# Attention weights and u turned by TensorE instead of by transposing transfers, with ScalarE, VectorE and GpSimd sharing the rest differently

## The chip, the cores and the metric

The kernel runs on one core of one Trainium2 chip. The metric is device time in microseconds. TensorE (PE in the profile) multiplies and turns matrices and writes to PSUM. VectorE (DVE), ScalarE (ACT) and GpSimd (POOL) do the elementwise work. SyncE (SP) issues transfers. Each engine takes its instructions in the order in which the program gives them.

## The reference, cut to what matters

```python
# q, k, v: (8 batches, 8 heads, 576 rows, 64), fp32; tau = 0.02
scores = scale * np.matmul(q, k.transpose(0, 1, 3, 2))          # 576 x 576 for each head
thresh = np.max(scores, axis=-1, keepdims=True) - tau
scores = np.where(scores >= thresh, scores, -1000000000.0)
scores = scores - np.max(scores, axis=-1, keepdims=True)
attn = np.exp(scores)
attn = attn / (np.sum(attn, axis=-1, keepdims=True) + 1e-09)
x = np.matmul(attn, v)                                          # heads side by side: (8, 576, 512)

xt = x.transpose(0, 2, 1)
h = xt @ U @ V                                                  # U: 576 x 32, V: 32 x 576
u = x + h.transpose(0, 2, 1)
ch = np.maximum(u @ w_ch1, 0.0) @ w_ch2                         # 512 x 2048 and 2048 x 512
out = u + ch
```

## The kernel before

There are eight batches of four pairs of heads, 32 pairs in all. The rows of a head are five tiles (four of 128 and one of 64; the short tiles of two pairs are put together), so that two pairs are nine steps, and the whole is 144 steps of two tiles each, 288 tiles of attention weights.

**Loads and preparation.** Each pair's q and k are loaded (L510), turned by TensorE in fp32 (L572, L585) and copied to `qkT` by ScalarE (L578, L591). `LOADERS` says for the first pairs which queue issues the loads; GpSimd issues the others. The values are split in bf16: ScalarE makes the high part `vh` (L600), GpSimd the low part (L607).

**A step.** TensorE multiplies scores for two heads, two steps at a time after the first pairs (L641), into the two tiles `trio` of PSUM, which hold six of its eight banks. For each of the two tiles VectorE scales and copies the scores to SBUF and takes their extreme (L670). ScalarE makes the threshold of both tiles, the extreme plus tau (L686), and the exponentials (L693). VectorE selects what passes the threshold and sums it up (L700), with the weights in bf16 going into `w_ring`. GpSimd copies 64 columns of a tile to fill a whole block (`twin`, L718). Then the tile, 128 x 640, must be turned for the product with the values. This is done in one of two ways:

- by a transposing transfer on SP's queue (`turn_w`, L724), of two tiles at a time, or one where the other goes the second way;
- by TensorE, five passes of 128 x 128 into a bank of PSUM (`turn_pe`, L731), and a copy to SBUF by ScalarE (`copy_w`, L741). So it is for 25 tiles: the second tile of steps 1 to 3 of the first eight pairs (`EARLY`), and one other.

`w_ring` holds four steps.

**A pair.** The turned tiles `wT_ring` and `wT4` are multiplied with `vh` (L800, L804, L808), the results put together by ScalarE and VectorE (L855, L859) and divided by the sums on GpSimd (L866). The first four pairs (`SOFT`) have one product with the inverse sums instead, on VectorE (L831). The inverse of the sums is two instructions of VectorE (L774 adds 1e-9, L776 inverts). Then follow the low-rank part (L871 to L885, L894), the sum u on VectorE (L901), its rounding to bf16 on ScalarE (L908), and the turning of u into `uT`: for the first eight pairs by TensorE (L916) with a copy by ScalarE (L932), for the other 24 by a transposing transfer on SP's queue (L922).

**A batch.** `mixer_tasks` multiplies `uT` with the first weight (`up`, L998, and `rest`, L1014), ScalarE takes the positive part (L988), TensorE multiplies with the second weight (`down`, L1031), and VectorE adds u from PSUM to SBUF (`finish`, L1043), from where it is sent out (L1054 to L1060).

**The order.** Every operation is a task, and the list `ORDER` gives the sequence in which the tasks are issued, `BANK` the PSUM bank of each that needs one. Negative numbers in `ORDER` are fillers, matmuls of an identity whose result is not used (L473). Costs and due times in the tasks served to make the lists; when the kernel is built, only the lists count:

```python
        for n in ORDER:
            if n < 0:
                self.filler(-1 - n)
                continue
            t = self.tasks[n]
```

Of the kernel before, what the change touches and what calls it, by code (L numbers as in the profile page):

```python
# [68 lines left out]
P = 128  # L69
FP32 = mybir.dt.float32  # L70
# [15 lines left out]
EARLY = 8  # L86
PHASES = (1, 2, 3, 4, 5, 6, 8, 28)
LONE = 2
LOADERS = (None, "SSSS", "SSSS")
ACTED = 0  # L90


W1_AT = (1, 4, 6, 9, 11, 14, 16, 19)
W2_AT = (20, 21, 23, 24, 25, 26, 28, 29)
# [14 lines left out]
PE, VEC, SCA, POOL, SP = range(5)  # L109
# [3 lines left out]
class Task:  # L113
# [17 lines left out]
    23, 21, 22, 25, 20, 26, 24, 19, 44, 28, 46, 40, 27, 29, 42, -1, -1, -1, -1, -1, -1, -1, -1, -1, 32, 41, 30, 33,  # L131
    43, 34, 31, 39, 35, 45, -2, -2, -2, 59, 201, 36, 200, 60, 37, 38, 204, 61, 63, -7, -7, -7, -7, -7, 69, 205, 62,
    65, 64, 206, 54, 70, 50, 198, 55, 52, 71, 203, 73, 218, 82, 66, 72, 202, 77, 222, 74, 199, 1, 83, 47, 67, 3, 84,
    49, 86, -3, -3, -3, -3, -3, -3, 95, 0, 78, 68, 85, 51, 87, 53, 90, 96, 75, 97, 219, 76, -8, -8, -8, -8, -8, -8,
    108, 91, 221, 98, 99, 2, 48, 211, 103, 109, 207, 209, 110, 112, 119, 100, 225, 212, 111, 104, 79, 114, 213, 120,
    92, 224, -3, 80, 121, 123, 220, -7, 129, 115, 125, 223, 113, 122, 4, 93, 131, 432, 56, 130, 101, 210, 88, 439,
    142, 89, 124, 137, 105, 81, 126, 57, 106, 102, 94, 143, 169, 132, 127, 144, 437, 146, 128, 155, 168, 214, 150,
    138, 107, 233, 170, 139, 231, 116, 157, 145, 438, 133, 117, 229, 156, 232, 457, 238, 134, 163, 455, 208, 151,
    158, 234, 171, 434, 230, 240, 159, 135, 58, 136, 239, 140, 244, 147, 152, 241, -6, 248, 141, 118, 172, 456, 242,
    245, 5, 243, 433, 153, 249, 453, 154, 250, 160, -8, -8, -8, -8, 173, 251, 164, 215, 161, 174, 256, 452, 261, -1,  # L140
    -1, -1, 184, 162, 148, 252, 262, 435, 264, 183, 149, 165, -4, 273, 257, 459, 175, 185, 246, 258, 253, 247, 216,
    274, 176, 254, 458, 275, 228, 177, 263, 268, 217, 286, -8, -8, 178, 255, 166, 259, 281, 179, 443, 454, 277, 269,
    188, 226, 436, 276, 287, 444, 227, 6, 180, 189, 265, 167, -3, -3, -3, -3, -3, -3, 181, 278, 288, 266, 289, 296,
    282, 270, 260, 267, 182, 290, 283, 291, 297, 441, 279, 271, 186, 292, 280, 300, 298, 272, 293, 345, 235, 440,
    344, 187, 299, 306, 294, 236, 302, 447, 445, 237, 307, 284, 448, 309, 346, 308, 301, 626, 446, 462, -2, -2, -2,
    318, 285, 303, 295, 190, 310, 304, 460, 313, 319, 191, 320, 9, 192, 322, -8, -8, 193, 331, 311, 347, 326, 624,
    312, 194, 321, 620, 334, 314, 349, 305, 195, 467, 348, 315, 625, 350, 468, 332, -4, 316, 351, 465, 333, 339,
    352, 335, 463, 353, 466, 196, 323, 336, 354, 317, 472, 355, 324, 464, 619, 325, 327, 356, 337, 622, 197, 474,
    357, 328, 338, 442, 623, 473, 364, 358, 461, 621, 329, 340, 475, 476, 482, 639, 359, 478, 341, 477, 640, 330,
    365, 8, 483, 342, 484, 360, 10, 343, 495, 7, 486, 362, 496, 449, 642, 479, 485, 507, 469, 363, 487, 490, 470,  # L150
    361, 498, 509, 480, 634, 366, 488, 481, 630, 471, 508, 632, 635, 631, 521, 367, 644, 633, 489, 520, 368, 497,
    511, -7, -7, 369, 491, 530, 522, 510, 370, 515, 492, 645, 499, 371, 887, 502, 531, 882, 372, 374, 532, 373, 12,
    493, 375, 494, 641, 380, 503, 533, 523, 376, 540, 504, 381, 11, 505, 525, 516, 378, 500, 377, 512, 886, 501,
    382, 506, 526, 450, 379, 384, 383, 541, 534, 13, 386, 524, 536, 513, 552, 535, 527, 514, 385, 537, 542, 883,
    387, 543, 528, 517, 538, 553, 646, 518, 547, 650, 554, 451, 519, 388, 529, 566, 555, 14, 390, 628, 565, 389,
    888, 651, 659, 544, 391, 556, 545, 884, 392, 546, 660, 560, 661, 394, 567, 568, 629, 548, 393, 669, 647, 561,
    395, 549, 539, 572, 557, 643, 665, 670, 562, 550, 558, 663, 648, 16, 396, 671, 551, 627, 885, 573, 398, 397,
    569, 672, 400, 662, 399, 682, 570, 673, 574, 402, 571, 881, 683, 401, 563, 674, 403, 652, 559, 654, 564, 578,
    577, 901, 598, 653, 666, 15, 655, 649, 575, 677, 694, 664, 579, 678, 685, 667, 580, 689, 679, 695, 581, 892,
    576, 696, 902, 684, 894, 698, 18, 707, 896, 582, 893, 690, 675, 897, 702, 586, 708, 676, 583, 599, 895, 584,  # L160
    587, 636, 585, 588, 717, 668, 686, 903, 600, 601, 589, 710, 691, 637, 712, 718, 17, 607, 590, 719, 603, 687,
    638, 697, 727, 608, 709, 680, 703, 656, 591, 904, 889, 692, 404, 699, 604, 907, 592, 890, 681, 609, 704, 406,
    602, 605, 688, 693, 728, 606, 405, 593, 765, 713, 906, 407, 723, 711, 908, 739, 766, 610, 594, 700, 611, 657,
    767, 701, 714, 595, 905, 740, 612, 658, 715, 912, 752, 613, 720, 596, 729, 614, 721, 741, 1048, 705, 911, 408,
    734, 1054, 722, 716, 597, 1049, 409, 724, 706, 1051, 753, 410, 742, 747, 725, 615, 1055, 726, 411, 730, 735,
    913, 914, 412, 743, 736, 769, 1053, 731, 915, 413, 616, 773, 744, 732, 770, 916, 737, 774, 748, 917, 617, 1072,
    755, 733, 921, 775, 754, 749, 764, 738, 771, 794, 776, 909, 618, 923, 768, 750, 795, 414, 922, 745, 759, 772,
    746, 796, 1068, 924, 415, 760, 751, 1071, 925, 891, 756, 931, 1050, 927, 926, 1052, 777, 785, 757, 932, 1075,
    786, 758, 933, 1070, 941, 778, 761, 934, 787, 416, 779, 942, 935, 780, 788, 898, 417, 781, 944, 928, 762, 950,
    763, 936, 929, 937, 418, 797, 782, 930, 899, 951, 946, 790, 789, 952, 900, 910, 960, 1063, 1059, 791, 954, 1061,  # L170
    792, 1057, 961, 783, 793, 943, 420, 1062, 1056, 938, 1069, 953, 784, 421, 1280, 947, 1064, 1060, 939, 970, 956,
    945, 1278, 940, 798, 955, 948, 957, 918, 949, 799, 962, 971, 919, 422, 800, 965, 1277, 972, 806, 1058, 974, 801,
    1073, 966, 423, 963, 1074, 807, 426, 958, 802, 920, 808, 959, 427, 981, 803, 1279, 973, 424, 428, 985, 1273,
    980, 804, 809, 964, 429, 805, 976, 975, 967, 811, 982, 810, 430, 1009, 968, 983, 986, 977, 989, 1010, 1078, 812,
    1011, 978, 1008, 1274, 979, 990, 1083, 1079, 991, 993, 969, 1013, 984, 1080, 425, 995, 813, 999, 987, 1014,
    1000, 843, 992, 988, 1084, 814, 1015, 1001, 1017, 996, 1002, 1088, 994, 1065, 1018, 1004, 1066, 1081, 1019,
    1003, 1016, 815, 1082, 1089, 844, 1037, 1020, 1090, 819, 997, 1038, 998, 1039, 1091, 1005, 816, 817, 1094, 1006,
    1098, 1076, 1012, 1092, 1095, 1293, 1007, 818, 1093, 1295, 820, 1021, 1099, 1275, 821, 431, 1276, 1100, 1022,
    822, 1298, 1029, 1028, 1077, 1108, 1023, 1104, 1067, 1024, 1109, 823, 1030, 1101, 1031, 1102, 1096, 1281, 1296,
    1105, 1117, 824, 1097, 1294, 1103, 1110, 1113, 1299, 1025, 1111, 1106, 1282, 1297, 1118, 1288, 1284, 1107, 1300,  # L180
    1119, 1289, 1286, 1285, 1127, 1033, 1441, 1287, 1128, 1123, 1040, 845, 1112, 1034, 1120, 1085, 1137, 1035, 1124,
    846, 1121, 1114, 1026, 1139, 1115, 825, 1129, 1447, 1130, 1116, 1138, 1036, 827, 1143, 1122, 1032, 826, 829,
    1148, 1140, 1141, 1125, 831, 1442, 1147, 1126, 830, 1086, 1131, 828, 847, 832, 1149, 1156, 1132, 1142, 1041,
    1133, 848, 1157, 1134, 1150, 1308, 1087, 1135, 1042, 1158, 1309, 1304, 1043, 1152, 1166, 1306, 1176, 1305, 1027,
    1167, 1467, 1307, 1175, 1440, 1168, 1044, 1151, 1159, 833, 1283, 1177, 1443, 1178, 1302, 1313, 1446, 1144, 834,
    1303, 1160, 1045, 1145, 1180, 1466, 1146, 1315, 1465, 1314, 835, 1181, 1445, 1169, 1153, 1323, 1461, 1162, 1161,
    1179, 1316, 1182, 836, 1163, 1171, 1184, 1324, 1319, 1164, 1444, 1204, 1325, 1185, 1317, 837, 1154, 1464, 1170,
# [186 lines left out]
def kernel(  # L374
# [24 lines left out]
    nc.vector.tensor_copy(out=identb, in_=ident)  # L399
    tau_t = consts.tile([P, 1], FP32, name="tau_t")  # L400
    nc.vector.memset(tau_t, tau_f)

    warm = consts.tile([P, 1], FP32, name="warm")
    nc.scalar.activation(out=warm, in_=tau_t, func=ACT.Exp)

# [761 lines left out]
```

## Time and profile before

| | |
|---|---|
| runs of the kernel | 602.58 and 609.11 us, median 605.85 us |
| profiled execution | 601.79 us, span 600.0 us |
| PE busy | 574.2 us, 96% of the span |
| DVE busy | 515.7 us, 86% |
| ACT busy | 459.4 us, 77% |
| POOL busy | 337.1 us, 56% |
| granted TensorE clock | full in all 40 slices |
| transfers issued on SP's queue that turn tiles or u | 167: 127 to `wT_ring`, 16 to `wT4`, 24 to `uT` |
| packets of the queue that carries them | 212544, 69.2% of the time of the 16 DMA engines |

The span runs from the first instruction to the last, and the device time contains a little more. Busy shares are of the span. Matmuls overlap on PE, so that a busy PE can have room, and the time of a stretch of matmuls is better read from the distance of their starts than from the length of one.

### The profile page before, as it was taken

How to read it: one execution, taken by the hardware profiler on the slowest of the kernel's cores; microseconds unless marked ns; L12 is line 12 of the kernel's file. 1: busy time of each engine (PE TensorE's matmuls, PEld its weight loads, DVE VectorE, ACT ScalarE, POOL GpSimd, SP SyncE). 2: the span in 40 equal slices, each digit the busy share in tenths (PEclk: the TensorE clock that was granted, in tenths of full speed). 3: DMA queues.
4: the chain of work that ended last, by engine and by line, in shares of the span. 5: the costliest groups of instructions: out<-in, count | busy, mean ns of one | idle time of the engine just before them, and what ended most of it. 6: DMA issues, size and time to landing. Idle time of an engine off the chain costs nothing. (4 is left out here: it accounts for less than half of the span.)

```text
span 600.0 us, 16926 instructions
## 1 busy us (share of the span) xinstructions
PE 574.2 (96%) x6150; PEld 346.3 (58%) x6221; DVE 515.7 (86%) x1399; ACT 459.4 (77%) x959; POOL 337.1 (56%) x580
## 2 busy tenths in 40 slices
PE   7999999899999998999999999999999999999996
PEld 4466655665665664656565665556655666555542
DVE  3999999999999999999999999999988999962002
ACT  3788999898898876997679986799786887683330
POOL 2987777787467558664567474576473544141000
PEclk9999999999999999999999999999999999999999
DMA  5999999986999899998898998998999877684203
GB/s 118 177 159 153 177 156 183 167 173 136 155 164 168 156 173 177 175 160 155 162 176 159 170 154 184 192 167 167 157 174 142 176 135 138 97 155 74 62 19 88
DMA packets 226996, 90.49 MB, mean 151 GB/s; under 512 B 205408, under 2 KB 217520, under 8 KB 226912
## 3 DMA queue, kind: packets, MB, share of 16 engines
q1 hardware_dynamic: 212544, 67.48, 69.2%
q0 software_dynamic: 13408, 21.58, 17.7%
q8 instruction: 49, 0.80, 0.6%
q10 hardware_dynamic: 960, 0.34, 0.2%
q14 instruction: 35, 0.29, 0.2%
HBM read 37.90 MB, written 9.44 MB: 79 GB/s over the span
## 5 line engine op out<-in xcount | busy, mean ns | idle before, releaser
L693 ACT ACTIVATE e_sb<-s_sb,m 128x576 bf16<-128x576 f32 x288 | 216.4, 776 | 37.6 <-DVE w_ring L700 25.9
L700 DVE SCALAR_TENSOR_TENSOR w_ring<-s_sb,thr,e_sb 128x576 bf16<-128x576 f32 x288 | 236.9, 849 | 6.4 <-DMA wT_ring<-w_ring 2.7
L670 DVE TENSOR_SCALAR_CACHE_REDUCE s_sb<-trio 128x576 f32<-128x576 f32 x288 | 205.9, 751 | 13.4 <-PE trio L641 11.3
L641 PE MATMUL trio<-qkT 64*64 64x288 f32 (+2 forms) x2304 | 162.3, 410 | 2.0 <-DVE s_sb L670 1.7
L718 POOL COPY w_ring<-w_ring 128x128 bf16<-128x128 bf16 (+1 forms) x168 | 67.8, 410 | 127.5 <-DVE w_ring L700 85.9
L641 PEld LDWEIGHTS trio<-qkT 64*64 64x64 f32 x2304 | 82.4, 132 | 57.9 <-issue 7.3
L1031 PEld LDWEIGHTS <-R 128*128 128x128 bf16 x576 | 53.5, 98 | 65.8 <-issue 12.1
L1031 PE MATMUL bank<-W2b,R 128*128 128x512 bf16 x338 | 84.6, 379 | 3.8 <-DVE o L1043 1.9
L510 POOL DMA_DIRECT2D qkraw<-in_q_dram x117 | 76.9, 659 | 10.0 <-PE bank L572 3.0
L510 POOL DMA_DIRECT2D qkraw<-in_k_dram x117 | 76.4, 655 | 10.7 <-PE bank L572 6.3
L998 PEld LDWEIGHTS <-W1b 128*128 128x128 bf16 x512 | 47.0, 98 | 53.6 <-issue 3.8
L866 POOL TENSOR_TENSOR x<-x,rec 128x256 f32<-128x256 f32 (+1 forms) x84 | 55.0, 660 | 38.4 <-DVE x L859 24.8
L607 POOL TENSOR_TENSOR vh<-vraw_ring,vh 64x128 bf16<-64x128 f32 (+1 forms) x64 | 54.0, 843 | 23.1 <-ACT vh L600 11.3
L998 PE MATMUL trio<-uT,W1b 128*128 128x512 bf16 x256 | 62.3, 379 | 1.4 <-ACT tt L885 0.4
L804 PEld LDWEIGHTS <-wT_ring 128*128 128x128 bf16 x896 | 55.7, 98 | 10.0 <-issue 6.1
L998 PE MATMUL bank<-uT,W1b 128*128 128x512 bf16 x223 | 58.2, 379 | 0.9
L988 ACT ACTIVATE R<-trio 128x512 bf16<-128x512 f32 x74 | 41.9, 599 | 15.5 <-PE trio L998 13.5
L1031 PE MATMUL trio<-W2b,R 128*128 128x512 bf16 x200 | 47.6, 379 | 2.4 <-ACT R L988 1.9
L686 ACT ACTIVATE thr<-m,tau_t 128x2 f32<-128x2 f32 x144 | 41.5, 296 | 7.4 <-DVE s_sb L670 7.3
L988 ACT ACTIVATE R<-bank 128x512 bf16<-128x512 f32 x70 | 40.7, 595 | 5.2 <-PE bank L1014 3.3
L804 PE MATMUL bank<-vh,wT_ring 128*128 128x128 bf16 x512 | 36.6, 219 | 0.0
L1043 DVE TENSOR_TENSOR o<-trio,x 128x512 f32<-128x512 f32 x13 | 8.9, 690 | 31.3 <-PE trio L1031 31.3
(105 smaller groups left out, 731.4 us busy)
## 6 DMA issues: line engine op xcount, KB each, us to landing
out_dram<-o SPq DMA_DIRECT2D x71, 128.0 KB, 2.8
vraw_ring<-in_v_dram SPq DMA_DIRECT2D x32, 160.0 KB, 3.5
qkraw<-in_k_dram POOLq DMA_DIRECT2D x59, 80.0 KB, 3.9
qkraw<-in_q_dram POOLq DMA_DIRECT2D x58, 80.0 KB, 4.0
vraw_ring<-in_v_dram SPq DMA_DIRECT2D x32, 128.0 KB, 4.1
qkraw<-in_q_dram POOLq DMA_DIRECT2D x59, 64.0 KB, 4.0
qkraw<-in_k_dram POOLq DMA_DIRECT2D x58, 64.0 KB, 3.9
W1b<-in_moe_w_ch_dram POOLq DMA_DIRECT2D x8, 256.0 KB, 5.0
```

Of the source, the lines that this page charges most:

```text
L510: queue.dma_start(pr.qkraw[part, to, j, :], src[:, j, of, :])
L607: nc.gpsimd.tensor_tensor(out=pr.vh[part, tiles_, :, h, :], in0=raw[part, tiles_], in1=pr.vh[part, tiles_, :, 0, :], op=ALU.subtract)
L641: mm = nc.tensor.matmul(cols[part, lo:hi], a.tT[hs, 0, rows], a.tT[hs, 1, lo:hi], start=True, stop=True)
L670: nc.vector.tensor_scalar(out=s_sb, in0=score_cols(slot, x), scalar1=-scale, scalar2=None, op0=ALU.mult, op1=ALU.min, accum_out=m[:, x:x + 1])
L693: nc.scalar.activation(out=e_sb, in_=s_sb, func=ACT.Exp, bias=m[:, x:x + 1], scale=-1.0)
L700: nc.vector.scalar_tensor_tensor(out=w_sb[:, 0:S], in0=s_sb, scalar=thr_[:, x:x + 1], in1=e_sb, op0=ALU.is_le, op1=ALU.mult, accum_out=pr. ...
L718: nc.gpsimd.tensor_copy(out=w_sb[:, xs, S:640], in_=w_sb[:, xs, 512:S])
L804: nc.tensor.matmul(av[:, 2 * a + j, :], w, pr.vh[:, kt, j, :, :], start=kt == 0, stop=False)
L866: nc.gpsimd.tensor_tensor(out=x, in0=x, in1=over_sum(part), op=ALU.mult)
L988: nc.scalar.activation(out=R2[:, fts, lo:hi], in_=bank[t.got[0]].rearrange("p (f c) -> p f c", c=hi - lo), func=ACT.Relu)
L998: nc.tensor.matmul(bank[t.got[0]], W1b[:, dt, ft * P:(ft + 1) * P], bt.uT[:, dt, :], start=(dt == 0), stop=(dt == 3))
L1031: nc.tensor.matmul(ch, R2[:, ft, lo:lo + P], W2b[:, ft, :], start=(ft == 0), stop=(ft == 15))
```

## The change

- Every weight tile is turned by TensorE, one at a time. Of each step's two tiles ScalarE copies the first out of PSUM and VectorE the second (`COPIED`). All blocks of u are turned by TensorE, too, and copied by ScalarE. No transposing transfer is left.
- GpSimd makes the high part of the values (`HIGH`) and the threshold (`THRESH`) for all pairs, in place of ScalarE.
- ScalarE adds 1e-9 to the sums, in place of VectorE. For the first four pairs (`ACTED`) ScalarE takes the products out of PSUM and GpSimd divides them, in place of one instruction of VectorE.
- For the first seven batches (`SHARED`) the last sum is a copy out of PSUM by ScalarE and an addition by GpSimd, in place of VectorE's addition.
- Pairs 1 to 6, not 1 and 2, have their q and k loaded from SP's queue. The loads of the weights are tied to one another and not to scores.
- Some tasks name fewer tasks that they need: `up` only its half of the first weight, `down` only its quarter of the inputs.
- `ORDER` and `BANK` are new lists. There are 44 fillers in place of 56. The lists themselves and declarations are left out below.

```diff
-EARLY = 8
+COPIED = (SCA, VEC)
-LOADERS = (None, "SSSS", "SSSS")
-ACTED = 0
+LOADERS = (None,) + ("SSSS",) * 6
+SHARED = 7
+THRESH = 32
+HIGH = 32
+ACTED = 4
...
-        t = done["vhi", p] = add(SCA, 0.62, high,
+        def top(_):
+            nc.gpsimd.tensor_copy(out=pr.vh[:, :, :, 0, :], in_=raw)
+        t = done["vhi", p] = add(*(POOL, 1.1, top) if p < HIGH else (SCA, 0.62, high),
...
-        thr = add(SCA, 0.19, threshold, mins)
+        def level(_):
+            nc.gpsimd.tensor_scalar(out=thr_, in0=m, scalar1=tau_f, scalar2=None, op0=ALU.add)
+        thr = add(POOL, 0.2, level, mins, lock=0.03) if p < THRESH else add(SCA, 0.19, threshold, mins)
...
-            both = not (p < EARLY and 1 <= i < 4)
-            if both and not x:
-                first_sel = sel
-                tiles[0] += 1
-                done.setdefault(("den", p), []).append(sel)
-                continue
-            def twin(_, xs=slice(0 if both else x, x + 1)):
+                              got("den4", p - 3)], lock=0.08)
+            def twin(_, x=x):
                 w_sb = w_ring[n % (NW // 2)]
-                nc.gpsimd.tensor_copy(out=w_sb[:, xs, S:640], in_=w_sb[:, xs, 512:S])
-            twin_ = add(POOL, 0.235 if both else 0.18, twin, [sel] + ([first_sel] if both else []), lock=0.03)
-            def turn_w(_, xs=slice(0 if both else x, x + 1)):
-                to = pr.wT[:, xs, :, i * P:(i + 1) * P] if i < 4 else wT4[:, xs, :, HB:HB + P]
-                nc.sync.dma_start_transpose(
-                    to.rearrange("p x k r -> p (x k) r"),
-                    w_ring[n % (NW // 2)][:, xs, :].rearrange("p x c -> p (x c)"))
+                nc.gpsimd.tensor_copy(out=w_sb[:, x, S:640], in_=w_sb[:, x, 512:S])
+            ready = add(POOL, 0.18, twin, [sel], lock=0.03)
             def turn_pe(t, w_sb=w_ring[n % (NW // 2)][:, x, :]):
                 ps = bank[t.got[0]][:, 0:320].bitcast(BF16)
...
             free = [got("AV", p - 2, c) for c in range(2)] if i < 4 else \
                 [got("AV", a, 2) for a in (p - 2, p - 1)]
-            if i < 4 and (x == 1 and p < EARLY and i >= 1 or p == NPAIR - 1 and i == 3):
-                t = done["wT", tiles[0]] = add(PE, 0.28, turn_pe, [twin_] + free, banks=1,
-                                               kind="wT")
-                def copy_w(_, x=x, t=t):
-                    nc.scalar.copy(
-                        out=pr.wT[:, x, :, i * P:(i + 1) * P],
-                        in_=bank[t.got[0]][:, 0:320].bitcast(BF16).rearrange(
-                            "p (k r) -> p k r", k=NT))
-                t = add(SCA, 0.575, copy_w, [t], frees=[t])
-            elif both:
-                t = done["wT", tiles[0]] = done["wT", tiles[0] - 1] = add(
-                    SP, 1.44, turn_w, [twin_] + free, dma=2.2)
-            else:
-                t = done["wT", tiles[0]] = add(SP, 1.28, turn_w, [twin_] + free, dma=1.1)
+            t = done["wT", tiles[0]] = add(PE, 0.28, turn_pe, [ready] + free, banks=1, kind="wT")
+            def copy_w(_, x=x, t=t, on=nc.vector.tensor_copy if COPIED[x] == VEC else nc.scalar.copy):
+                on(out=pr.wT[:, x, :, i * P:(i + 1) * P] if i < 4 else wT4[:, x, :, HB:HB + P],
+                   in_=bank[t.got[0]][:, 0:320].bitcast(BF16).rearrange("p (k r) -> p k r", k=NT))
+            t = add(COPIED[x], 0.42 if COPIED[x] == VEC else 0.575, copy_w, [t], frees=[t])
...
+        def guard(_):
+            nc.scalar.activation(out=pr.rec, in_=pr.den, func=ACT.Identity, bias=eps_t[:, 0:1], scale=1.0)
         def inverse(_):
-            nc.vector.tensor_scalar(out=pr.rec, in0=pr.den, scalar1=1e-9, scalar2=None,
-                                    op0=ALU.add)
             nc.vector.reciprocal(out=pr.rec, in_=pr.rec)
-        rec = done["rec", p] = add(VEC, 0.335, inverse, done["den", p] + [got("den4", p), got("xb", p - 4)], lock=0.03)
+        rec = add(SCA, 0.19, guard, done["den", p] + [got("den4", p), got("xb", p - 4)])
+        rec = done["rec", p] = add(VEC, 0.17, inverse, [rec])
...
         deps = [ub] + done.get(("p1", pr.b - 2), [])
-        def send_u(_):
-            nc.sync.dma_start_transpose(
-                bt.uT[:, pr.hp, :].rearrange("p (t r) -> p t r", t=4),
-                pr.ub.rearrange("p t c -> p (t c)"))
-        if p < EARLY:
-            uT_ = done["uT_", p] = add(PE, 0.23, turn_u, deps, banks=1, kind="uT")
-        else:
-            done["uT_", p] = done["uT", p] = add(SP, 1.3, send_u, deps, dma=0.9)
+        uT_ = done["uT_", p] = add(PE, 0.23, turn_u, deps, banks=1, kind="uT")
         def copy_u(_):
             nc.scalar.copy(out=bt.uT[:, pr.hp, :], in_=bank[uT_.got[0]][:, 0:256].bitcast(BF16))
-        if p < EARLY:
-            done["uT", p] = add(SCA, 0.478, copy_u, [uT_, got("uT", p - 1)], frees=[uT_])
+        done["uT", p] = add(SCA, 0.478, copy_u, [uT_, got("uT", p - 1)], frees=[uT_])
...
-            t = add(PE, 0.862, up, uT + weights1 + done.get(("o", b - 2), []), banks=1, kind="p1",
+            t = add(PE, 0.862, up, uT + weights1[ft // 8 * 4:ft // 8 * 4 + 4] + done.get(("o", b - 2), []), banks=1, kind="p1",
...
-                halves.append(add(PE, 0.865, down, (relus4 if i == 4 else relus) + weights2 + (
+                halves.append(add(PE, 0.865, down, (relus4[g:g + 1] if i == 4 else relus[4 * g:4 * g + 4]) + weights2[2 * g:2 * g + 2] + (
                     halves or [got("down")]), banks=int(not g), kind="ch", when=when))
...
-            t = done["sum"] = add(VEC, 0.603, finish, [halves[-1], outs[0], got("sum")],
-                                  frees=[halves[0]])
+            def hold(_, halves=halves, o=o):
+                nc.scalar.copy(out=o, in_=bank[halves[0].got[0]])
+            def plus(_, i=i, o=o):
+                nc.gpsimd.tensor_tensor(out=o, in0=o, in1=bt.x[:, i, :] if i < 4 else bt.x4, op=ALU.add)
+            if b < SHARED:
+                t = add(SCA, 0.485, hold, [halves[-1], outs[0], got("sum")], frees=[halves[0]])
+                t = done["sum"] = add(POOL, 1.1, plus, [t, got("sum")], lock=0.03)
+            else:
+                t = done["sum"] = add(VEC, 0.603, finish, [halves[-1], outs[0], got("sum")],
+                                      frees=[halves[0]])
...
```

## The prediction

> **What bounds the kernel now.** I read the busy shares of the page first, then the busy time by stretches, then the chain of waits for the pace of each kind of matmul, then the groups of instructions for the operations that the change adds or drops.
>
> ```profile
> PE 574.2 (96%) x6150; PEld 346.3 (58%) x6221; DVE 515.7 (86%) x1399; ACT 459.4 (77%) x959; POOL 337.1 (56%) x580
> ```
>
> ```profile
> 0.00:60.00 60.00, 53.50 (x658) 31.94 (x658) 50.57 (x150) 43.06 (x84) 41.88 (x77) 1.00 0.91 152
> 60.00:120.00 60.00, 56.41 (x742) 36.38 (x742) 57.47 (x160) 56.74 (x118) 45.27 (x81) 1.00 1.10 171
> 120.00:330.00 210.00, 204.08 (x2265) 125.92 (x2292) 203.58 (x549) 173.59 (x371) 137.25 (x234) 1.00 0.93 164
> 330.00:540.00 210.00, 206.80 (x2182) 124.84 (x2210) 194.55 (x530) 169.76 (x359) 111.13 (x189) 1.00 0.92 158
> 540.00:600.00 60.00, 53.43 (x320) 27.21 (x325) 9.57 (x15) 16.28 (x33) 1.62 (x3) 1.00 0.31 61
> ```
>
> The columns are stretch, length, then busy time of PE, weight load, DVE, ACT and POOL, granted clock, DMA share and GB/s. PE and DVE are both nearly full until 540 us; after that DVE has 9.6 us of work in 60 and PE runs on alone. The clock is full throughout. But a busy PE is not a PE at its peak, because matmuls overlap. So I price its work by pace, from pieces of the chain that ended last (start, length, what, count):
>
> ```profile
> 465.68 2.10 PE trio L641 x32
> 484.69 1.73 PE bank L998 x8
> 488.78 0.44 PE bank L572 x4
> 490.55 0.28 PE trio L879 x5
> ```
>
> That is 0.0656 us for a score matmul, 0.216 for one of 512 columns, 0.11 for an fp32 transpose, 0.0555 for 128 bf16 columns. Times the counts that the code issues: scores 2304 x 0.0656 = 151; up 512 and down 576 of 0.216 = 234.5; rest 256 x 0.0555 = 14; values (L800, L804, L808) 83; q and k 31.5; low rank and its spreads 18; blocks of u 2.7; weight tiles 125 x 0.0555 = 7; 56 fillers 12. Sum **553 us of the 600**. So 47 us are idle, and the order of instructions says where. The first up matmul starts at 83.2 us; the work queued before it is 64 us at pace, so 19 us of the idle lie there (start, and the scores' wait for DVE, which is 99% busy from 30 to 90 us). From 83 us to the end it is 489.7 us of work in 517: only 27 us idle. **TensorE is the bound from the first mixer on.**
>
> **What is removed.** 143 transposing transfers of weight tiles (L724) and 24 of u (L922), on SP's queue. This is who waited for L724's transfers:
>
> ```profile
>   DVE w_ring L700: 2.7, 3
>   PEld L808: 2.0, 3
>   PE bank L808: 1.3, 2
> ```
>
> They take 4.7 us to land, but about 4 us of waiting is all that hangs on them. With them goes much of the DMA share of 0.9 to 1.1, which holds up nothing else in the table of waits. Gain: 0 to 4 us; I take none apart from the idle below.
>
> **What is added on TensorE.** All 288 tiles are now turned, five passes each, where 25 were; 24 more blocks of u at four passes; 12 fillers fewer. The operation is in the trace (start, length; weight loads, then passes):
>
> ```profile
> 27.43 0.28 PEld L731 LDWEIGHTS <-w_ring 128*128 128x128 bf16 x5 [0.44 <-issue]
> 27.44 0.45 PE L731 MATMUL bank<-identb,w_ring 128*128 128x128 bf16 x5
> L731 PE MATMUL bank<-identb,w_ring 128*128 128x128 bf16 x80 | 7.3, 220 | 0.5 <-POOL w_ring L718 0.3
> ```
>
> Five passes cost 0.28 us of engine time, though one lasts 220 ns. The Trainium skill ("TensorE: Matmul & The Clock Gate", Part 4: PE-mode transpose) gives a 128x128 transpose about 275 ns in a kernel and says that transposes don't count toward the full clock. By that rule 1315 + 96 more passes would be 388 us, a span near 990. The row decides: here they are pipelined at 0.0555 us, at clock 1.00. So 1315 x 0.0555 = 73.0, u 96 x 0.0555 = 5.3, fillers -2.6: **+75.7 us, 629 in all**. The skill's other page, "VectorE: DVE Perf Modes" (Rules for kernel authors; The three transpose paths), says to turn 128x128 tiles on TensorE where PSUM will do, and sets 390 ns against 1309 for the transfer. By it, 263 tiles of five blocks would gain; by this trace the transfer's time lies on a queue that hardly anyone waits for, and the shorter operation lies on the engine that is full. I follow the trace.
>
> **The other engines,** to see if one overtakes it.
>
> ```profile
> L741 ACT COPY wT_ring<-bank 128x640 bf16<-128x640 bf16 x16 | 11.0, 687 | 1.6 <-PE bank L731 1.6
> L686 ACT ACTIVATE thr<-m,tau_t 128x2 f32<-128x2 f32 x144 | 41.5, 296 | 7.4 <-DVE s_sb L670 7.3
> L600 ACT CAST vh<-vraw_ring 128x640 bf16<-128x640 f32 x32 | 23.1, 723 | 0.1
> L1043 DVE TENSOR_TENSOR o<-bank,x 128x512 f32<-128x512 f32 x23 | 15.7, 684 | 6.3 <-PE bank L1031 6.2
> L859 DVE TENSOR_TENSOR x<-bank,x 128x256 f32<-128x256 f32 x32 | 13.5, 421 | 2.1 <-ACT x L855 1.9
> L718 POOL COPY w_ring<-w_ring 128x64 bf16<-128x64 bf16 x48 | 18.3, 391 | 11.4 <-DVE w_ring L700 10.7 <-PE trio L572 0.2
> L607 POOL TENSOR_TENSOR vh<-vraw_ring,vh 128x512 bf16<-128x512 f32 x32 | 37.6, 1175 | 0.7
> ```
>
> *ScalarE:* +119 weight copies x 0.69 = 82, +24 copies of u x 0.58 = 14, +32 guards x 0.3 = 9.5, +31 copies of finished sums x 0.59 = 18, +12 takes = 4; thresholds -41.5, high parts -23. So 459 becomes 523.
> *VectorE:* +144 copies of 128x640 bf16 out of PSUM. No row shows one. L859 and L1043 give 1.03 ns an element and 0.16 us fixed, so 0.82 us at that rate is the upper end; two elements a cycle would give 0.49, the lower. I take 0.49, since both sides are 16-bit and the page on VectorE just named (Why PSUM operands drop a tier) lets such a source have a double rate; no run here shows it yet. +71 us (upper end 118), less 31 sums of 0.687 = 21, 32 additions = 7 and 12 products = 4: 516 becomes 554 (601).
> *GpSimd:* 288 single twins x 0.39 in place of 68 us = +45; 144 thresholds x 0.3 = +43 (0.39 at most); 32 high parts x 1.2 = +38; 31 late sums of 512 columns, twice L866's 0.718 less a start, 1.3 = +40; +12 products = 8; 32 fewer q and k issues x 0.66 = -21 (now SP's, whose queue has lost 167 transposing issues of 1.3 us). 337 becomes 490.
> Against a span near 680 these are 77, 81 (88) and 72%; TensorE's work is 93%. It stays the bound. In the stretch before the first up matmul TensorE gets 4.8 us more work (43 tiles instead of 14, fewer fillers). VectorE, tight there, gets 21 copies x 0.42 (busy less the overlap of 0.07 that L670's rows show) = 9, less 4.3 for products and additions: also +4.7.
>
> **The new waits.** A weight tile now passes select, GpSimd's twin, PE, PSUM, copy, value matmul. Behind a turn that is not ready waits everything queued on PE. A select waits for a threshold on GpSimd, which can stand behind one of 1.2 to 1.3 us; behind that select wait the next reductions, and the scores that need their banks. Uses of PSUM banks other than the scores' grow from 481 to 768. Against that, the other three engines have more slack than before. The lists that set every engine's order are new too, so a longer chain need not end as a wait of PE; but PE takes its work in order, and where a link comes late it stops. Bounds for the idle after the first up matmul: 10 us (slack wins) to 60 (it doubles); I leave it at its share of the work, 5.6%, between them.
>
> **Sum.** To the first up matmul 83.2 + 4.8 = 88. After it 629.1 - 68.5 = 560.6 of work; with the idle unchanged 588, in proportion 592; 590. The span is 678, with the 1.8 us that lie around the span (601.79 to 600.0) **680 us**, against 601.8 for the profiled execution. The two runs shown have a median of 605.85, 4 us above it, and spread by 6.5; I don't add that, but the range allows it. A change of about 2% either way is what this measurement can tell from none.
>
> **Rivals.**
> 1. *VectorE becomes the bound* (copies at 0.82 us). For: its density up to 540 us is 506 of 540, 94%. Against: both sides are 16-bit. Then 597 us at 94% are 635, and the last mixer's 60 to 70 us of PE follow: about 700.
> 2. *PE starves* for late tiles or for banks. For: 60% more bank uses, thresholds behind long GpSimd work. Against: only 77 to 81% load elsewhere. Idle 60 instead of 29: 710.
> 3. *Tighter than now*: idle 10, 660; with the start's idle gone as well 650.
> 4. *Not slower*: the passes fall into gaps that PE has anyway. It would need the price of a tile to sink. Of 600 us some 16 (start, end) can't be filled, and the work without the added tile passes is 556; 28 us remain for 263 tiles, 0.106 us each. From there down it is no slower, about 600. L731's 0.28 speaks against it, and it is the same pace as L879's. That the tiles aren't turned on PE at all is excluded by the instruction order: 1440 passes.
>
> **How the numbers follow.** Forecast 0.74 (its own range 660 to 700), VectorE 0.09, starving 0.12, tighter than 660 0.03, not slower 0.02. The likeliest gives 680. The range takes in both slow rivals' centres and the lower idle: 654 to 715. Faster by over 2% 0.01, within 2% 0.01, slower 0.98.
>
> **What would show it.** Right: 1440 PE passes on the tiles five in 0.28 us, PE dense from about 88 us on, the last scores near 590 us (now 525), DVE copies near 0.49 us, none of the other engines over 90%. Wrong: copies of 0.8 us and DVE full; many long PE waits for copies, twins or thresholds; passes much nearer or farther apart than 0.0555 us.

## The result, and the profile after

The changed kernel takes **693.8 us** (693.08 and 694.51), against 605.85 before: ratio 1.145 [1.118, 1.172]. A repeat with four runs of it beside seven of the kernel before gave 694.34 against 604.11, 1.149 [1.146, 1.152]. It is slower. The forecast was 680, with a range of 654 to 715. The profiled execution took 694.51 us, its span 692.6.

The page's line of busy times, after:

```profile
PE 656.4 (95%) x7535; PEld 425.1 (61%) x7620; DVE 560.7 (81%) x1469; ACT 523.2 (76%) x1001; POOL 461.7 (67%) x887
```

PE has 82 us more than before, DVE 45, ACT 64, POOL 125. The next view gives busy time by stretches, in the columns of the prediction (stretch, length, PE, weight load, DVE, ACT, POOL, granted clock, DMA share, GB/s):

```profile
0.00:60.00 60.00, 52.30 (x692) 33.17 (x693) 51.18 (x142) 39.15 (x72) 35.04 (x80) 1.00 0.68 119
120.00:330.00 210.00, 202.58 (x2409) 134.58 (x2439) 189.92 (x502) 170.90 (x328) 161.82 (x306) 1.00 0.24 61
330.00:540.00 210.00, 204.10 (x2399) 136.21 (x2428) 181.37 (x475) 169.54 (x329) 158.35 (x301) 1.00 0.24 64
615.00:692.00 77.00, 72.00 (x509) 39.54 (x515) 17.34 (x35) 37.63 (x74) 16.02 (x22) 0.99 0.21 45
```

The DMA share has fallen from 0.9 to 0.24: the transposing transfers are gone. The clock is 0.99 to 1.00. From 120 to 540 us PE reads as full as before, while DVE is a little less full (371 us of 420, before 398). This looks like the forecast: TensorE is the fullest engine, with VectorE at 88% behind it. The page also follows the work that ended last back, step by step, to what released it, and gives the engines' shares of this chain ("issue" is time in which an engine waited for nothing that the profile shows). It says something else. First after, then before:

```profile
PE 31%; DVE 11%; ACT 3%; issue 3%; POOL 2%; DVEq 0%; POOLq 0%; ACTq 0%
```

```profile
PE 23%; ACT 1%; DVE 1%; issue 0%
```

The chain could be followed through half of the span only (through a quarter before), so that it proves little; but in that half DVE, ACT and POOL have 16 of 50 points. One kernel of the experiments shows PE with nearly all of the chain; this one does not. The timeline shows the turn of three tiles in a row (start, length):

```profile
303.69 0.73 PE L773 MATMUL bank<-identb,w_ring 128*128 128x128 bf16 x10
304.26 0.44 PE L773 MATMUL trio<-identb,w_ring 128*128 128x128 bf16 x5
```

Ten passes start within 0.57 us, and the next five follow at once: 0.057 us each, the 0.0555 of the forecast. And these are the groups that the forecast priced (busy, mean ns; then idle before, and what ended it):

```profile
L755 DVE SCALAR_TENSOR_TENSOR w_ring<-s_sb,thr,e_sb 128x576 bf16<-128x576 f32 x288 | 249.0, 889 | 15.1 <-ACT e_sb L748 5.3 <-POOL thr L742 4.3 <-ACT uT L959 1.9
L781 ACT COPY wT_ring<-trio 128x640 bf16<-128x640 bf16 x69 | 47.5, 695 | 5.4 <-PE trio L773 4.7 <-DVE wT_ring L781 0.2
L781 DVE COPY wT_ring<-trio 128x640 bf16<-128x640 bf16 x65 | 31.2, 482 | 10.2 <-PE trio L773 6.4 <-ACT wT_ring L781 2.1 <-ACT e_sb L748 0.7
L766 POOL COPY w_ring<-w_ring 128x64 bf16<-128x64 bf16 x288 | 93.6, 341 | 87.9 <-DVE w_ring L755 75.0 <-PE trio L696 3.5 <-PE bank L914 2.5
L1076 POOL TENSOR_TENSOR o<-o,x 128x512 f32<-128x512 f32 x31 | 40.3, 1303 | 20.2 <-ACT o L1073 19.9
L742 POOL TENSOR_SCALAR thr<-m 128x2 f32<-128x2 f32 x144 | 49.5, 344 | 54.4 <-DVE s_sb L725 42.7 <-DMA vraw_ring<-in_v_dram 2.8
```

The copy out of PSUM takes VectorE 0.48 us, ScalarE 0.69. The select, which the change does not touch, takes 889 ns where it took 849. This is its row before:

```profile
L700 DVE SCALAR_TENSOR_TENSOR w_ring<-s_sb,thr,e_sb 128x576 bf16<-128x576 f32 x288 | 236.9, 849 | 6.4 <-DMA wT_ring<-w_ring 2.7 <-ACT thr L686 1.6 <-POOL w_ring L718 0.7
```

### The profile page after: what moved, and what is told of

Same layout as the page of the kernel before. It is cut to its first block, busy times and chain, and to the rows that moved or that the text cites. A ratio compares the mean times of both kernels' runs of the same rounds, so it can differ in the third digit from the quotient of the medians.

```text
span 692.6 us, 19769 instructions
## 1 busy us (share of the span) xinstructions
PE 656.4 (95%) x7535; PEld 425.1 (61%) x7620; DVE 560.7 (81%) x1469; ACT 523.2 (76%) x1001; POOL 461.7 (67%) x887
## 3 DMA queue, kind: packets, MB, share of 16 engines
q1 hardware_dynamic: 36320, 23.58, 14.6%
## 4 chain that ended last, share of the span: by engine, by line
PE 31%; DVE 11%; ACT 3%; issue 3%; POOL 2%; DVEq 0%; POOLq 0%; ACTq 0%
PE trio L1057 6%; DVE w_ring L755 5%; PE trio L696 5%; PE bank L1057 5%; DVE s_sb L725 4%; PE trio L1024 3%; PE bank L1024 3%; PE trio L839 2%; PE trio L773 2%; PE bank L773 1%; ACT e_sb L748 1%; PE bank L839 1%; ACT R L1014 1%; PE trio L1040 1%; PE trio L625 1%
## 5 line engine op out<-in xcount | busy, mean ns | idle before, releaser
L755 DVE SCALAR_TENSOR_TENSOR w_ring<-s_sb,thr,e_sb 128x576 bf16<-128x576 f32 x288 | 249.0, 889 | 15.1 <-ACT e_sb L748 5.3
L766 POOL COPY w_ring<-w_ring 128x64 bf16<-128x64 bf16 x288 | 93.6, 341 | 87.9 <-DVE w_ring L755 75.0
L773 PEld LDWEIGHTS <-w_ring 128*128 128x128 bf16 x1440 | 91.9, 98 | 49.0 <-issue 17.6
L742 POOL TENSOR_SCALAR thr<-m 128x2 f32<-128x2 f32 x144 | 49.5, 344 | 54.4 <-DVE s_sb L725 42.7
L1057 PE MATMUL trio<-W2b,R 128*128 128x512 bf16 x304 | 74.9, 379 | 1.8 <-ACT R L1014 0.6
L773 PE MATMUL trio<-identb,w_ring 128*128 128x128 bf16 x780 | 66.1, 219 | 5.5 <-POOL w_ring L766 3.2
L563 POOL DMA_DIRECT2D qkraw<-in_q_dram x101 | 67.3, 668 | 5.1 <-PE trio L625 3.0
L1024 PE MATMUL bank<-uT,W1b 128*128 128x512 bf16 x251 | 67.7, 379 | 1.1
L1057 PE MATMUL bank<-W2b,R 128*128 128x512 bf16 x236 | 61.1, 379 | 1.2 <-issue 0.2
L773 PE MATMUL bank<-identb,w_ring 128*128 128x128 bf16 x660 | 56.6, 219 | 2.3 <-ACT x L870 0.9
```

The source lines that it names most:

```text
L563: queue.dma_start(pr.qkraw[part, to, j, :], src[:, j, of, :])
L755: nc.vector.scalar_tensor_tensor(out=w_sb[:, 0:S], in0=s_sb, scalar=thr_[:, x:x + 1], in1=e_sb, op0=ALU.is_le, op1=ALU.mult, accum_out=pr. ...
L766: nc.gpsimd.tensor_copy(out=w_sb[:, x, S:640], in_=w_sb[:, x, 512:S])
L773: nc.tensor.transpose(ps[:, kt * P:(kt + 1) * P], w_sb[:, kt * P:(kt + 1) * P], identb)
L1024: nc.tensor.matmul(bank[t.got[0]], W1b[:, dt, ft * P:(ft + 1) * P], bt.uT[:, dt, :], start=(dt == 0), stop=(dt == 3))
L1057: nc.tensor.matmul(ch, R2[:, ft, lo:lo + P], W2b[:, ft, :], start=(ft == 0), stop=(ft == 15))
```

## The experiments

They ask three things: do the passes make the added time, do the copies, or does the rest (where work lies and in what order)? Beside experiments 1 to 4 the kernel before took 604.11 us, beside 5 to 7 606.13, beside 8 and 9 606.12. Where two experiments of different groups are compared, these 2 us are left open, and the difference is given as a range. Ratios are to the kernel before, with 95% intervals.

**1. The repeat,** the changed kernel as it is. 

> The changed kernel once more, beside the others on the same chip, so that they have a neighbour. Every theory: 691 to 695 us.

694.34 us, 1.149 [1.146, 1.152].

**2. The passes alone, in the old kernel and its order.** As many passes as the transfers' tiles and blocks of u would need stand ahead of the matmuls that use them, on a constant.

```diff
             def product(t, tiles_=tiles_):
+                for i in tiles_:
+                    for j in range(2):
+                        turned = i < 4 and (j == 1 and p < EARLY and i >= 1 or p == NPAIR - 1 and i == 3)
+                        for kt in range(0 if turned or i == 4 and p % 2 else NT):
+                            nc.tensor.matmul(bank[t.got[0]][:, 0:P], identb, identb,
+                                             start=True, stop=True)
...
+            for i in range(4 if p >= EARLY else 0):
+                nc.tensor.matmul(bank[t.got[0]][:, 0:P], identb, identb, start=True, stop=True)
```

> The kernel before with the passes alone: for every weight tile that a transfer turns, TensorE makes five passes of 128 columns on an identity, in the bank of the value product just ahead of it, and for every block of u that a transfer turns four in the bank of the low-rank product; their results are overwritten. Transfers, copies and all else stay. TensorE-work theory (the loss is 1411 passes at 0.0555 us on a full engine): +78 us, 677 to 688. Rival (the loss comes from the waits that turning on TensorE brings, banks, copies, twins, thresholds): here none of these is added, so less than +40, under 645. Rival (passes fill gaps): 600 to 615.

672.22 us against 604.11, ratio 1.112 [1.108, 1.115]: **+68 us**, where 78 us of passes (1411 x 0.0555) were added; the other 10 us must have found idle time. This is the page's chain by engine for it:

```profile
PE 89%; ACT 4%; DMA 2%; issue 2%; DVE 1%; POOL 1%; SPq 1%; DVEq 0%; POOLq 0%; ACTq 0%
```

Here TensorE is the bound, and here it shows. The passes are enough by themselves for three quarters of the loss, and most of them don't fit into gaps.

**3. The changed kernel without its passes.** The copies read the unturned tile; all else is as it was.

```diff
-                for kt in range(NT):
-                    nc.tensor.transpose(ps[:, kt * P:(kt + 1) * P],
-                                        w_sb[:, kt * P:(kt + 1) * P], identb)
+                return
...
-                   in_=bank[t.got[0]][:, 0:320].bitcast(BF16).rearrange("p (k r) -> p k r", k=NT))
+                   in_=w_sb.rearrange("p (k r) -> p k r", k=NT))
```

> The changed kernel without the passes on weight tiles: the copies read the unturned tile from SBUF in place of PSUM, so the turning is left out. Thresholds, high parts, late sums, twins, copies and their order stay. TensorE-work theory: the work falls by 80 us to 549, so 605 to 622. Rival (the other engines' new load and the longer chains are the price): stays over 650.

**691.4 us**, 1.144 [1.140, 1.148]: 80 us less work on TensorE bring 3 us, hardly to be told from none. One thing blurs this: the granted clock was 0.980 to 0.989 in its four runs, against 0.995 to 0.999 in the repeat's, and the run with the highest clock was the shortest (687.25 us). By an estimate from these clocks, 2% of 690 us, this hides at most 14 us, not 80. Its page:

```profile
PE 589.5 (86%) x6107; PEld 346.1 (50%) x6180; DVE 561.3 (82%) x1469; ACT 523.3 (76%) x1001; POOL 466.8 (68%) x887
...
DVE 19%; PE 17%; ACT 10%; POOL 7%; issue 6%; DMA 1%; SPq 0%; POOLq 0%; DVEq 0%; ACTq 0%
```

PE falls to 86%, and what can be followed of the chain runs over DVE, PE, ACT and POOL by turns. My theory, one bound, predicted 605 to 622. It fell here.

**4. Is it the wait for a tile at its turn?** The passes stay, on a constant in place of the tile.

```diff
-                                        w_sb[:, kt * P:(kt + 1) * P], identb)
+                                        identb, identb)
```

> The changed kernel with the same 1440 passes in the same banks, but on an identity in place of the weight tile, so that the tile's turning is left out and no pass waits for a select or a twin. Theory that the idle beyond the sum (41 us after the first up matmul, 29 taken) is waiting for the tile at the turn: 10 to 18 us less than the changed kernel, 676 to 684. Rival (PE waits for banks and for scores that VectorE has not taken, because GpSimd holds up VectorE's selects): within 5 us of the changed kernel.

690.0 us, 1.142 [1.140, 1.144], 4 us less. So a select or a twin that comes late for the turn costs about that much.

**5. Ten passes a tile in place of five.** `range(NT)` becomes `range(2 * NT)`, with `kt %= NT`. 

> The changed kernel with each weight tile's five passes made twice over. TensorE-work theory: 1440 more passes at 0.0555 us on the full engine, +80 us, 768 to 780. Rival (the passes lie in gaps or wait on others anyway): under +40, below 735.

751.77 us, 1.241 [1.235, 1.247]: +55 to 57 us for 80 us of passes. So TensorE is close to being the bound without being it alone: 80 us less bring 3, 80 more cost 55 or more.

**6. GpSimd's new work given back.** The late sums return to VectorE (`hold` calls `finish`, `plus` does nothing); in a second kernel thresholds and high parts return to ScalarE (`THRESH = 0`, `HIGH = 0`). 

> The changed kernel with the last sums of the first seven batches on VectorE again, one instruction out of PSUM at the place of ScalarE's copy, in place of that copy and GpSimd's addition of 1.3 us. Theory that GpSimd's instructions with two inputs hold up VectorE's selects and through them PE: 3 to 6 us faster, 687 to 690. Theory that TensorE's work alone counts: within 2 us. Rival (VectorE is short of time): slower by 5 us or more.

> The changed kernel with thresholds and high parts on ScalarE again, each at its place in the order. ScalarE gains 65 us of work (84% of the span), GpSimd loses 74. Theory that thresholds on GpSimd come late or that GpSimd holds up VectorE's selects: 4 to 10 us faster, 683 to 690. TensorE's work alone: within 3 us. Rival (ScalarE, with both, becomes late for PSUM): 5 to 15 us slower.

The sums: 692.48 us, 1.144 [1.139, 1.148], not to be told from the change. Thresholds and high parts: 704.36, 1.163 [1.159, 1.167], 8 to 10 us slower; ScalarE's share goes from 76 to 80%. So in this order the move of these two to GpSimd is a gain.

**7. No twin on GpSimd.** The last 64 columns are turned twice, into the two halves of a block.

```diff
-                nc.gpsimd.tensor_copy(out=w_sb[:, x, S:640], in_=w_sb[:, x, 512:S])
+                return
...
-                for kt in range(NT):
+                for kt in range(NT - 1):
...
+                for half in range(2):
+                    nc.tensor.transpose(ps[HB * half:HB * half + HB, (NT - 1) * P:NT * P],
+                                        w_sb[:, 512:S], identb)
```

> The changed kernel without twins: in place of GpSimd's copy of 64 columns, TensorE turns the last 64 columns of a tile twice, into the lower and the upper half of the block, six passes a tile, the last two of them 64 wide. 94 us of GpSimd's work and one link between select and turn go. If the two narrow passes run side by side or cost by half: 0 to 14 us faster (679 to 694). If each costs 0.0555 us, 288 x 0.0555 = +16 on the full engine, less what the link gives: 694 to 708.

736.95 us, 1.217 [1.212, 1.221]: 41 to 43 us slower, which no theory had. The timeline of PE in it:

```profile
300.79 0.39 PE L773 MATMUL bank<-identb,w_ring 128*128 128x128 bf16 x4
301.11 0.25 PE L776 MATMUL bank<-identb,w_ring 128*64 128x128 bf16 x2
301.29 0.40 PE L842 MATMUL trio<-vh,wT_ring 128*128 128x128 bf16 x4
```

Four full passes should take 0.22 us, but the narrow ones start 0.32 after them, and the next full ones 0.18 later: 0.50 us a tile, not 0.28. Over the trace's 288 tiles the medians are the same (317 and 176 ns), while the two narrow passes start 3 ns apart, side by side. Over 288 tiles this is 63 us of TensorE's time, of which 41 to 43 show. So the kernel settles nothing about GpSimd's twin; it shows the price of narrow weights between wide ones.

**8. The copies, in the changed kernel.** They move 40 of 640 columns; in one kernel with the passes, in the other without, where they read the unturned tile. (Left out: the turned tiles are filled with zeros once at the start.)

```diff
-                on(out=pr.wT[:, x, :, i * P:(i + 1) * P] if i < 4 else wT4[:, x, :, HB:HB + P],
-                   in_=bank[t.got[0]][:, 0:320].bitcast(BF16).rearrange("p (k r) -> p k r", k=NT))
+                on(out=pr.wT[:, x, :, i * P:i * P + 8] if i < 4 else wT4[:, x, :, HB:HB + 8],
+                   in_=bank[t.got[0]][:, 0:320].bitcast(BF16).rearrange("p (k r) -> p k r", k=NT)[:, :, 0:8])
```

> The changed kernel with its passes, but each copy of a turned tile takes only 40 of its 640 columns (the rest of the turned weights stay zero from the start, so most of the tile is left out of the result). It takes some 40 us from VectorE and 55 from ScalarE. The kernel without passes ran in 691 us, so the passes are not the only thing that holds it there. Theory of two limits of equal height, TensorE's work and the chain of elementwise engines with the copies in it: no more than 20 us faster, 670 to 692, since the passes alone hold it up. Theory that only the copies count: 640 to 655. Theory that the order itself holds everything: 688 to 695.

> The changed kernel without the passes and with copies of 40 columns, so that the turning is left out whole. Theory of two limits: with both gone, 610 to 645. Theory that the order, or GpSimd's thresholds, high parts and late sums, hold it: 665 or more.

With passes 688.77 us, 1.134 [1.131, 1.138]; without them **676.94**, 1.116 [1.113, 1.119]. So less copying brings 6 to 9 us, and less copying without passes 17 to 20. Here is VectorE's copy without passes, which reads `w_ring` in SBUF:

```profile
L781 DVE COPY wT_ring<-w_ring 128x40 bf16<-128x40 bf16 x128 | 35.4, 289 | 0.2
```

It saved VectorE less than I had meant (289 ns are left of 480). With the 16 copies to `wT` (558 ns each) VectorE still copies for 44 of its 69 us, so this kernel took only 16 us off VectorE's busy time; it took 66 off ScalarE and 80 off TensorE. The clock was 0.981 to 0.990. Even so: with the passes and most of ScalarE's copying gone, 71 us of the loss remain. They lie in what was left: the order, GpSimd's share and VectorE's remaining copies.

**9. The copies, in the old kernel and its order.** Each tile is copied in place ahead of its transfer, first tiles by ScalarE, second by VectorE; once alone, once with the passes of experiment 2.

```diff
             def turn_w(_, xs=slice(0 if both else x, x + 1)):
+                for x_ in range(xs.start, xs.stop):
+                    on = nc.vector.tensor_copy if x_ else nc.scalar.copy
+                    w = w_ring[n % (NW // 2)][:, x_, :].rearrange("p (k r) -> p k r", k=NT)
+                    on(out=w, in_=w)
```

> The kernel before with copies alone: for every tile that a transfer turns, a copy of its 640 columns onto itself just ahead of the transfer, by ScalarE for the first tile of a step and by VectorE for the second. No pass, and nothing else of the change. VectorE gets 120 x 0.48 = 58 us more (575 us), ScalarE 143 x 0.72 = 103 (562). Theory that VectorE and ScalarE are as near to the bound as TensorE: 640 to 665. Theory that only TensorE counts: under 620.

> The kernel before with the passes of the run of passes alone (672 us) and the copies of the run of copies alone. If the two costs lie side by side: near the larger of the two, 672 to 690. If they add up: 710 or more.

Copies alone: **647.4 us**, 1.067 [1.065, 1.070], +41. With the passes: **692.57**, 1.141 [1.138, 1.145], 18 to 20 more than with the passes alone. These are the added copies of the first kernel:

```profile
L727 DVE COPY w_ring<-w_ring 128x640 bf16<-128x640 bf16 x120 | 51.1, 425 | 1.9 <-POOL w_ring L718 1.8
L727 ACT COPY w_ring<-w_ring 128x640 bf16<-128x640 bf16 x143 | 103.5, 724 | 7.8 <-POOL w_ring L718 7.2
```

They stand in for the change's copies but are not the same: they stay in SBUF, where VectorE needs 425 ns and not 483, and they lie between twin and transfer. These are the page's chains of the first and of the second kernel:

```profile
PE 15%; ACT 11%; DVE 8%; issue 4%; DMA 2%; POOL 1%; SPq 0%; ACTq 0%; POOLq 0%; DVEq 0%
```

```profile
PE 54%; ACT 21%; DVE 10%; DMA 8%; issue 6%; POOL 0%; SPq 0%; ACTq 0%; DVEq 0%; POOLq 0%
```

So the copies, which I had taken to add nothing to the end, cost 41 us, without one pass added. And the kernel before, with passes and copies put in, is within 1% of the whole change; what else the change does nets to nothing there, which may be a sum of gains and losses.

The five kernels that matter, split at their last score: before, after, experiment 3 (no passes), experiment 9 with copies alone, and with both. One fence for each, columns as above.

```profile
0.00:524.20 524.20, 505.15 (x5712) 310.42 (x5778) 495.12 (x1352) 429.44 (x900) 328.75 (x566) 1.00 0.95 161
524.20:600.00 75.80, 69.07 (x442) 35.86 (x443) 20.62 (x48) 29.99 (x60) 8.40 (x14) 1.00 0.41 79
```

```profile
0.00:603.10 603.10, 572.82 (x6916) 377.93 (x6990) 536.39 (x1417) 477.12 (x912) 439.82 (x852) 1.00 0.29 68
603.10:692.60 89.50, 83.62 (x627) 47.15 (x630) 24.28 (x53) 46.04 (x90) 21.84 (x36) 0.99 0.19 41
```

```profile
0.00:596.70 596.70, 510.12 (x5569) 303.68 (x5635) 535.33 (x1415) 476.60 (x911) 443.81 (x851) 0.99 0.29 68
596.70:685.40 88.70, 79.39 (x542) 42.41 (x545) 25.97 (x56) 46.68 (x90) 22.99 (x37) 0.99 0.20 42
```

```profile
0.00:569.00 569.00, 521.80 (x5716) 313.11 (x5778) 530.99 (x1466) 508.77 (x1037) 330.04 (x566) 1.00 0.84 149
569.00:645.70 76.70, 69.41 (x442) 35.70 (x443) 22.81 (x54) 33.04 (x66) 7.55 (x14) 1.00 0.40 78
```

```profile
0.00:609.90 609.90, 582.44 (x7040) 384.83 (x7111) 530.19 (x1468) 511.64 (x1037) 327.18 (x566) 1.00 0.80 139
609.90:691.10 81.20, 73.68 (x520) 40.07 (x521) 22.69 (x54) 33.28 (x66) 7.53 (x14) 0.99 0.36 74
```

The third and the fourth load TensorE and VectorE nearly alike: no added passes, 288 and 263 copies, VectorE 535 and 531 us busy before the last score; ScalarE has 32 us less there in the third, GpSimd 114 more. Yet the changed kernel's form is 40 us longer, 28 of it before the last score and 12 after. Its lower clock (0.989 against 0.997) can make at most 6 of these, by an estimate from the two figures. So its new order, GpSimd's share and the other differences together cost about 40 us where no passes stand in the stream, and nothing where they do (second and fifth: 692.6 and 691.1). A reading that fits, and is not shown: the passes fill time that the new order leaves open anyway. In the old order the same passes cost 68 us alone and 45 on top of the copies.

## Why the prediction was right, and where it was not

**The sizes held.** The passes run at 0.0555 us each. TensorE's work of 629 us: the instruction lists and the pace give the same. First up matmul at 91.2 us (88 forecast). DVE copies 0.483 us (0.49 taken of 0.49 to 0.82). ScalarE 523 (523), VectorE 561 (554), GpSimd 462 (490: a high part took 0.77, not 1.2, and a twin 0.34, not 0.39). That the end of the transfers brings nothing was not tried by itself.

**The trace decided rightly against the rule** that a transposing pass takes about 275 ns in a kernel and does not count toward the full clock (the Trainium skill, "TensorE: Matmul & The Clock Gate", Part 4): a span near 990 was not seen, and the mean clock was 0.999. Turning on TensorE, which the page "VectorE: DVE Perf Modes" (Rules for kernel authors) prefers, lost here, as the prediction said: the passes alone cost 68 us (experiment 2).

**The term that was mis-sized** was the idle after the first up matmul: 692.6 - 91.2 - 560.6 = 40.8 us, not 29.4, inside the bounds of 10 to 60. With 3.2 us at the start this is the whole difference of 14.6 between span and forecast. I had left the idle at its share of the work, 5.6%; it rose to 7.3%.

**The step that failed** is "It stays the bound", with copies that cost nothing because the other engines have shares of 77, 81 and 72%. Those shares are of the whole span, with the last 75 us in which only TensorE has much to do. Up to the last score the kernel before has DVE busy for 495 of 524 us, 94%; TensorE's work by pace there is 553 less the 68.5 that its list has behind the last score, 484.5, 92%. So there were two limits of nearly equal height, not one, and the change loads both. The forecast had the 94%, but used it only in the rival with the dear copy. Experiment 9 gives what it left out: copies 41 us alone, 18 to 20 on top of the passes. Passes and copies together cost 86 us in the old order; the whole change costs 88 to 90. The forecast had 76 for the passes and nothing for the copies. That it came near is in part luck: the passes were 8 us cheaper than forecast, and the copies, overlapping with them, cost 18 to 20 and not 41.

**The last scores** were forecast near 590 and came at 603.1, with 89.5 us after them where there were 75.8. Of that, the order itself has a part: by count and pace, 83.2 us of TensorE's work stand behind the last score in the new list, against those 68.5 in the old; 4.7 of the difference are 85 passes. Without the passes the end is still 88.7 us.

**The rivals.** VectorE as the bound at 0.82 us a copy: the price was wrong; the place was not far off (94% busy up to the last score), but VectorE alone was not shown to be the bound. Starving: few long waits for tiles, 4 us by experiment 4. Tighter than now: no, the idle grew. Passes in gaps: refuted by experiment 2 for the old order; for the new one, experiment 3 makes passes nearly free, but the gaps came with the change.

**What stays open.** Without passes, and with copies cut to 40 columns, the changed kernel still needs 677 us. How this divides between the order of the lists, GpSimd's load and VectorE's remaining copies was not settled. Nor was it settled whether VectorE's or ScalarE's copies make the 41 us of experiment 9: before the last score VectorE was 94% busy in the kernel before and 93% with the copies (531 of 569 us), ScalarE 82 and 89%, so VectorE is the likelier, but neither copy was tried alone. Two pieces of GpSimd's part can be read in the kernel of 677 us (who waited for what; total us, times, longest):

```profile
DVE w_ring L757 <- POOL thr L744: 14.2, 16, 2.5
```

VectorE stood 14 us for thresholds, and its selects took 907 ns against 849 before, 288 x 0.058 = 17 us. That these 31 us would all return is not shown: in the same order, thresholds and high parts on ScalarE made the change slower (experiment 6), and new lists were not tried. No version here beats the kernel before.

## What to carry to other kernels

Take busy shares over the stretch in which the engines work together, not over the span: an engine at 86% of the span was at 94% of what counted, and where a second engine is nearly full, price what the edit adds to that one too (here 68 and 41 us apart, 86 together). When the order on every engine is fixed in advance, taking work away from one engine can show little of its cost (80 us gone, 3 us back); put the work into the old order instead, piece by piece and together. A slow transfer can be cheap where hardly anyone waits for its queue: here 4.7 us to land, and some 4 us of waiting in all.

## What the runs showed of the hardware

- GpSimd's work slows some of VectorE's instructions. One select of the changed kernel and one GpSimd instruction at that time, from the timeline:

```profile
157.08 2.44 DVE L755 SCALAR_TENSOR_TENSOR w_ring<-s_sb,thr,e_sb 128x576 bf16<-128x576 f32 x1 [0.48 <-POOL w_ring L766]
```

```profile
157.73 1.17 POOL L660 TENSOR_TENSOR vh<-vraw_ring,vh 128x512 bf16<-128x512 f32 x1
```

  The select took 2.44 us, with a GpSimd instruction of two inputs inside its time. Over the whole traces, selects with no GpSimd instruction beside them took 811 ns on average, before (60 of 288) as after (53), and none over 821. All that took more than 1.2 us, 6 before and 21 after, had a two-input instruction or a conversion (CAST) of GpSimd beside them. A long select meets more by its length alone, so a trial says more than this count: where GpSimd's new work was taken back (experiment 6), the mean fell from 889 (881 in the repeat) to 860 (without the sums) and 857 (without thresholds and high parts). The total load alone does not set it: experiment 7 has 912 ns with 389 us of GpSimd's work.
- Not every VectorE instruction is slowed. In the change, copies out of PSUM took 482 ns with no GpSimd instruction beside them and 483 with one. Copies of 640 columns in place in SBUF (experiment 9, copies alone) took 317 ns without one (31 of 120) and 463 with one. The 40-column copies out of SBUF of experiment 8 took 161 and 337 ns, those out of PSUM about 170 either way.
- With no GpSimd instruction beside it, a VectorE copy of 640 columns took 317 ns in place in SBUF, but 473 from SBUF into the five pieces of a turned tile; why was not tried. This is the row of the latter, with and without GpSimd beside it (experiment 3):

```profile
L779 DVE COPY wT_ring<-w_ring 128x640 bf16<-128x640 bf16 x128 | 59.3, 474 | 0.7 <-POOL w_ring L766 0.3
```

- Weights of 64 columns between weights of 128 cost TensorE about 0.1 us at the change to them (0.32 less 4 x 0.0555), and 0.07 to 0.12 at the change back (0.18 less two passes or, as they run side by side, one; experiment 7).
